# Heads 6 and 7 as a fourth tile, one chunk's k from TensorE, one chunk's 1/rms from GpSimd: a change to a fused linear-attention and feed-forward kernel

## The chip, the cores and the metric

The kernel runs on one core of one Trainium2 chip. The time is the device time of the execution in microseconds (us), as the median of several runs. The granted clock is the share of its full clock that TensorE was given; over a whole profiled run it was 0.992 for the kernel before.

The engines' names in the profile are PE (TensorE, matmul), PEld (TensorE's weight load), DVE (VectorE), ACT (ScalarE), POOL (GpSimd) and SP (SyncE, which issues most of the DMAs). "L92" stands in every line, because one helper records every operation; groups are told apart by the tiles' names.

## The reference

```python
# attention: r, k, v (4, 8, 768, 48); w, u (8, 48)
state = zeros(B, H, D, D)
for t in range(S):
    cur     = einsum('bhd,bhe->bhde', u * k[t], v[t])
    y[t]    = einsum('bhd,bhde->bhe', r[t], state + cur)
    state   = w * state + einsum('bhd,bhe->bhde', k[t], v[t])
# bridge: (B,H,S,D) -> x (3072 tokens, 384)
rms = sqrt(mean(x * x, axis=-1) + 1e-6)
xn  = x / rms * rms_g
g   = xn @ w_gate                       # 384 x 1536
out = (g * sigmoid(g) * (xn @ w_val)) @ w_out   # 1536 x 384
```

## The kernel before

Time is cut into 12 chunks of 64 tokens for all 4 batches, and chunks go through the feed-forward part in pairs; a pair change is the passage from one pair to the next. Eight heads of 48 features give 384 rows. Before the change these were laid out as three tiles of 128 rows: two heads each, and in the rows 48 to 63 of each half a third of head 6 or 7.

```python
def outputs(bank, half):                     # PE; two halves of two batches per chunk
    py = bank[:, 0 : CC * 2 * L].rearrange("p (i t) -> p i t", i=CC)     # CC = 3
    for bl in range(2):
        ...
        for i in range(CC):
            for z, m in ((0, ME), (1, MO)):  # 16 rows of head 6 or 7
                pe.matmul(py[64*z : 64*z+64, i, cols], VS[:, z, b, at : at+L], m[:, b, 3, :], start=True, stop=False, ...)
            for z, m in ((0, ME), (1, MO)):  # 48 rows of heads 0 to 5, added
                pe.matmul(py[64*z : 64*z+D, i, cols], VS[:, z, b, i*D : (i+1)*D], m[:, b, i, :], start=False, stop=True, ...)
```

The result of a pair of chunks is four parts (`k`) of 128 rows. The rows 0 to 63 belong to one batch, the rows 64 to 127 to the next, and `j` counts the two pairs of batches. Before the change, a part was stored by two DMAs, one for each half of the rows. The list `ap` is the access pattern, a step and a count for each dimension, the slowest first:

```python
def result(k, chunk, f, js=(0, 1)):
    def give():
        for bl in range(2):
            to = bass.AP(tensor=out.tensor, offset=out.offset + ((2*js[0] + bl)*S + chunk*L)*DM + f*HALF,
                         ap=[[DM, L], [2*S*DM, len(js)], [1, HALF]])     # 64 tokens, 2 batches, 192 columns
            sp.dma_start(out=to, in_=results[bl*L : (bl+1)*L, k, js[0] : js[-1]+1])
    add("SP", 1.0, [f"r{k}"], [], give, name="store")
```

The steady part also looks at the weights a second time, to prove that they fit the range that the fast path handles. A check is a load of 384 KB into the tile `sq`, issued by SyncE, and two operations of ScalarE on it. There are 36 of them.

```python
def check(n, src, k):
    add("SP", 0.95, [], keys, lambda: sp.dma_start(out=raw, in_=src[:, k*CHECK : (k+1)*CHECK]), land=LAND, ...)
    add("ACT", 0.57, [], keys, lambda: act.activation(hi, hi, AF.Abs), ...)
    add("ACT", 0.81, [], keys + ["seen"], lambda: act.activation(hi, hi, AF.Relu, ..., accum_out=seen[:, n:n+1]), ...)
```

Every operation is entered in a plan with an assumed cost. The plan searches for a good order, and the instructions are emitted engine by engine in that order, so the order on each engine is fixed when the kernel is built. `LAND` (2.1) is what the plan takes for the landing of a load. In the gaps of TensorE in the first 27 us of the plan, dummy matmuls on ones are put in.

## Time and profile before

| | before |
|---|---|
| first three runs, median | 640.38 us (638.73 to 642.36) |
| profiled span | 638.1 us |
| TensorE busy / not busy | 619.1 / 19.0 us |
| last matmul to the end | 9.9 us |

The prediction below shows the page's head, TensorE's waits and its costly blocks. Two more views. First the DMA issues (what is written and read, queue, number of issues, KB each, median us from issue to landing):

```profile
sq<-in_wka_dram SPq DMA_DIRECT2D x12, 384.0 KB, 3.1
out_dram<-rows_out SPq DMA_DIRECT2D x46, 96.0 KB, 2.3
```

A check's load lands in 3.1 us and a store in 2.3. Second, the window in which most of the start lies (its start and end in us, its length, then busy time with instructions of PE, PEld, DVE, ACT and POOL, the granted clock, the DMA share and GB/s):

```profile
12.80:38.00 25.20, 19.28 (x372) 17.20 (x374) 22.36 (x32) 18.73 (x60) 4.38 (x5) 0.99 0.87 297
```

### The profile page before, as it was taken

Reading aid. Unit: us, or ns where it says so; the run is one execution under the profiler, and the core shown is the slowest. Engines: PE = TensorE matmul, PEld = TensorE weight load, DVE = VectorE, ACT = ScalarE, POOL = GpSimd, SP = SyncE. Lnnn points to the kernel's source line nnn. Section 1 sums busy time; section 2 is a strip of 40 time slices with the busy share of each in tenths; the row PEclk is TensorE's granted clock in tenths of the full one; section 3 lists DMA queues with packets and bytes.
Section 4 is the critical chain, followed back from the end, with each engine's and each line's share of the span. In section 5 each row is a group of like instructions: output and inputs, shape, how many; then the busy total and the mean of one; then the engine's idle time right before and its main releaser. Section 6 shows DMA issues by size and latency. Waiting matters only on the chain.

```text
span 638.1 us, 15980 instructions
## 1 busy us (share of the span) xinstructions
PE 619.1 (97%) x6880; PEld 550.2 (86%) x6880; DVE 437.3 (69%) x619; ACT 348.3 (55%) x914; POOL 41.2 (6%) x39
## 2 busy tenths in 40 slices
PE   9879999999999999999999999999999999999993
PEld 8767787887788899888899888899888899988993
DVE  7988869877676795478694568795468576455631
ACT  5696388763594256338858327958326952212200
POOL 3145212200000000000000000000000000000000
PEclk9989999999999999999999999999999999999997
DMA  8797372404351022252423241523241501100001
GB/s 270 262 314 251 123 237 54 146 2 140 96 164 30 7 89 73 75 161 78 141 92 99 52 160 52 167 73 95 75 142 46 140 5 49 26 2 1 2 13 43
DMA packets 21265, 64.54 MB, mean 101 GB/s; under 512 B 2752, under 2 KB 8512, under 8 KB 19776
## 3 DMA queue, kind: packets, MB, share of 16 engines
q1 hardware_dynamic: 21184, 63.42, 32.5%
q8 instruction: 56, 0.92, 0.6%
q14 instruction: 25, 0.20, 0.1%
HBM read 58.69 MB, written 4.72 MB: 99 GB/s over the span
## 4 chain that ended last, share of the span: by engine, by line
PE 87%; DMA 4%; DVE 3%; ACT 3%; issue 1%; POOL 0%; SPq 0%; DVEq 0%; POOLq 0%; ACTq 0%
PE bank_b L92 28%; PE bank_a L92 26%; PE bank_c L92 23%; PE at L92 11%; DMA chan<-in_chan_dram 3%; DVE bits L92 1%; ACT MO L92 1%; DVE rows_out L92 1%; DMA sq<-in_wot_dram 1%; DMA sq<-in_wka_dram 0%; ACT ME L92 0%; ACT sq L92 0%; DVE ME L92 0%; DVE chan L92 0%; ACT VS L92 0%
## 5 line engine op out<-in xcount | busy, mean ns | idle before, releaser
L92 DVE TENSOR_TENSOR gv<-bank_b,m 128x512 f32<-128x512 f32 x90 | 62.1, 690 | 70.6 <-PE bank_b L92 69.6
L92 PE MATMUL bank_b<-xa,wa 64*128 64x256 f32 x444 | 55.2, 381 | 2.0 <-POOL wa L92 1.5
L92 ACT ACTIVATE gv<-bank_a 128x256 f32<-128x256 f32 x30 | 11.5, 382 | 79.8 <-PE bank_a L92 79.7
L92 ACT ACTIVATE sq<-sq 128x384 f32<-128x384 f32 x72 | 40.4, 561 | 23.7 <-DMA sq<-in_wot_dram 11.8
L92 ACT ACTIVATE gv<-gv 128x256 f32<-128x256 f32 (+1 forms) x60 | 30.6, 521 | 37.0 <-DVE gv L92 36.6
L92 DVE TENSOR_TENSOR gv<-bank_c,gv 128x512 f32<-128x512 f32 x60 | 41.4, 689 | 12.2 <-PE bank_c L92 11.2
L92 PEld LDWEIGHTS bank_b<-xa,wa 64*128 64x128 f32 x444 | 42.0, 187 | 8.8 <-POOL wa L92 1.7
L92 PE MATMUL bank_a<-xa,wa 64*128 64x256 f32 x396 | 49.5, 382 | 0.1
L92 PE MATMUL bank_a<-wo,h 128*128 128x192 f32 (+1 forms) x264 | 49.4, 343 | 0.0
L92 PE MATMUL bank_a<-xb,wb 64*128 64x256 f32 x396 | 48.3, 377 | 0.0
L92 ACT ACTIVATE MO<-dmask,du 64x64 f32<-64x64 f32 x176 | 46.3, 336 | 1.3 <-DVE du L92 0.8
L92 PEld LDWEIGHTS bank_a<-wo,h 128*128 128x128 f32 x264 | 43.5, 190 | 3.7 <-issue 0.3
L92 ACT ACTIVATE ME<-dmask,du 64x64 f32<-64x64 f32 x176 | 45.5, 331 | 0.7
L92 PE MATMUL bank_b<-t,s 64*128 64x256 f32 x360 | 44.3, 378 | 0.5 <-DVE rows_out L92 0.5
L92 PE MATMUL bank_b<-t,wb 64*128 64x256 f32 x360 | 44.1, 377 | 0.2 <-DVE gv L92 0.2
L92 PE MATMUL bank_c<-xb,s 64*128 64x256 f32 x360 | 44.2, 378 | 0.0
L92 PE MATMUL bank_c<-t,s 64*128 64x256 f32 x360 | 44.0, 377 | 0.0
L92 PEld LDWEIGHTS bank_a<-xa,wa 64*128 64x128 f32 x396 | 37.3, 187 | 6.1 <-issue 1.4
L92 PEld LDWEIGHTS bank_a<-xb,wb 64*128 64x128 f32 x396 | 38.3, 187 | 4.7 <-issue 0.3
L92 ACT COPY m<-bank_a 128x512 f32<-128x512 f32 (+1 forms) x35 | 19.8, 566 | 40.7 <-PE bank_a L92 23.2
L92 PEld LDWEIGHTS at<-ME,VS 128*64 128x64 f32 (+1 forms) x576 | 35.3, 135 | 7.3 <-DVE MO L92 4.1
L92 PE MATMUL at<-ME,VS 128*64 128x64 f32 (+1 forms) x576 | 37.3, 226 | 3.7 <-DVE MO L92 3.7
(143 smaller groups left out, 1288.5 us busy)
## 6 DMA issues: line engine op xcount, KB each, us to landing
chan<-in_chan_dram SPq DMA_DIRECT2D x11, 1024.0 KB, 6.0
TOK<-in_tok_dram SPq DMA_DIRECT2D x12, 768.0 KB, 5.6
VS<-in_vpad_dram SPq DMA_DIRECT2D x24, 336.0 KB, 5.0
raw<-in_wot_dram SPq DMA_DIRECT2D x8, 576.0 KB, 4.4
sq<-in_wka_dram SPq DMA_DIRECT2D x12, 384.0 KB, 3.1
sq<-in_wkb_dram SPq DMA_DIRECT2D x12, 384.0 KB, 3.1
sq<-in_wot_dram SPq DMA_DIRECT2D x12, 384.0 KB, 3.1
out_dram<-rows_out SPq DMA_DIRECT2D x46, 96.0 KB, 2.3
```

Of the source, the lines that this page charges most:

```text
L92: return lambda *args, **kwargs: self.tc.keep_in_program_order(give(*args, **kwargs))
```

## The change

The intent is to shorten TensorE's stream. Heads 6 and 7 become a fourth tile, made by 8 matmuls a batch in place of 12, and a DMA (`move_heads`) brings their 16-row pieces to the rows where the feed-forward part expects them. Chunks 2 and 3 take the short way of the norm that chunks 4 to 11 had. In the start, chunk 0's k by tokens is made by TensorE from k by channels in place of being loaded, the dummy matmuls before the first real one become fewer, and chunk 1's 1/rms is a power on GpSimd in place of a square root on ScalarE. Some smaller things go with it: the search tries four seeds, the first part of an output projection is cut in two, P4 and P7 change places, and the stores are cut by `j` in place of by half.

```diff
 def outputs(bank, half):
-        for i in range(CC):
-            ... 16 rows of head 6 or 7 (start), then 48 rows (stop): 4 matmuls
+        for p in range(HP):                                   # HP = 4
+            for z, m in ((0, ME), (1, MO)):
+                pe.matmul(py[64*z : 64*z+64, p, bl*L : (bl+1)*L], VS[:, z, b, p*L : (p+1)*L],
+                          m[:, b, p, :], start=True, stop=True, skip_group_check=True)
+def move_heads(lo, hi):
+    for z in range(2):
+        sp.dma_start(out=yT[64*z+D : 64*z+64, :, lo:hi], in_=last_heads[64*z : 64*z+D, lo:hi])
...
+def turn_k(bank, half):                                       # chunk 0 only: 16 matmuls a half
+    pe.matmul(pk[64-64*z : 128-64*z, bl, p, :], CH[rows, 1, b, p, :], KH[rows, z, b, p, :], ...)
+def keep_k(bank, half, z):
+    act.copy(KH[rows, z, 2*half : 2*half+2], pk[rows])
...
-        quick, brief = s == 0, s > FIRST + 1
+        quick, early, turned, brief = s == 0, s < 1, s < 1, s > 1
...
+def power(y, x):                                              # chunk 1: GpSimd, then a step of Newton on DVE
+    pool.tensor_tensor(out=y, in0=x, in1=minus_half, op=ALU.pow)
...
-            for _ in range(int((until - since - 0.3) / 0.22) - (9 if since == 0 else 0)):
+            for _ in range(int((until - since - 0.3) / (0.22 if since else 0.5))):
...
 def result(k, chunk, f, js=(0, 1)):
-    for bl in range(2):
-        to = bass.AP(..., ap=[[DM, L], [2 * S * DM, len(js)], [1, HALF]])
-        sp.dma_start(out=to, in_=results[bl * L : (bl + 1) * L, k, js[0] : js[-1] + 1])
-    add("SP", 1.0, [f"r{k}"], [], give, name="store")
+    for j in js:
+        to = bass.AP(..., ap=[[S * DM, 2], [DM, L], [1, HALF]])   # 2 batches, 64 tokens, 192 columns
+        sp.dma_start(out=to, in_=results[:, k, j])
+    add("SP", 0.6 * len(js), [f"r{k}"], [], give, name="store")
```

## The prediction

> **What bounds the kernel now.** I first read the page's busy shares and then the waits of TensorE. The page:
>
> ```profile
> span 638.1 us, 15980 instructions
> PE 619.1 (97%) x6880; PEld 550.2 (86%) x6880; DVE 437.3 (69%) x619; ACT 348.3 (55%) x914; POOL 41.2 (6%) x39
> ```
>
> The waits of TensorE (who, for whom, total us, times, longest):
>
> ```profile
> PE at L92 <- DVE MO L92: 3.7, 1, 3.7
> PE at L92 <- DVE diag L92: 1.7, 2, 1.0
> PE bank_b L92 <- POOL wa L92: 1.5, 1, 1.5
> PE bank_c L92 <- DVE pw L92: 1.2, 1, 1.2
> ```
>
> Of a span of 638.1 us, TensorE (PE) is idle for 19. The listed waits and two of 0.6 and 0.5 give 9.2; the other 9.9 lie after its last matmul (628.2 us in the timeline), where the last results are stored and the program ends. So in the steady part PE never waits, and what leaves PE's instruction stream leaves the time. Only the start is different. There PE is "busy" partly with dummy matmuls on ones: by the groups 82 instructions, 13.4 us, all before 27 us.
>
> Next I read the chain that ended last in order of time, for the cost of whole blocks (start, us, what):
>
> ```profile
> 36.66 4.62 PE at L92 x95
> 46.66 1.43 PE at L92 x12
> 76.57 1.57 PE at L92 x64
> 84.82 2.04 PE at L92 x64
> 118.07 2.89 PE at L92 x96
> ```
>
> The x96 block is one chunk's outputs: the code issues 4 x 12 = 48 matmuls and the trace has two instructions for each. It costs 2.89 us, 30.1 ns an instruction. The x64 block of 2.04 is one chunk's scores, the one of 1.57 its state update (48 columns), the x12 its mean squares. The first line is the outputs of chunk 1: the same work took 4.62 us. The windows say why (columns: PE, weight load, DVE, ACT, POOL busy; granted clock, DMA share, GB/s):
>
> ```profile
> 30.00:34.00 4.00, 1.57 (x12) 1.08 (x12) 3.54 (x6) 3.96 (x18) 1.99 (x2) 1.00 0.98 311
> 34.00:38.00 4.00, 1.34 (x40) 1.34 (x42) 2.89 (x5) 3.93 (x15) 0.40 (x1) 0.96 1.01 382
> 38.00:42.00 4.00, 4.00 (x70) 3.84 (x68) 3.90 (x6) 3.92 (x9) 2.28 (x3) 0.61 0.82 269
> ```
>
> From 30 to 38 PE is mostly idle while ACT and DVE are full and DMA at its limit, and just afterwards the granted clock is 0.61. From 41.3 us on PE has next to no gap. So the time is **start (41.3) + PE work + 9.9**.
>
> **What the Trainium skill says.** (1) "TensorE: Matmul & The Clock Gate", Part 3 (row/col tiling): small matmuls at different tile positions run concurrently, the position following the operands' start partitions. The trace agrees: the even and the odd head's instruction start at most 0.01 us apart, pairs about 0.06 us apart, so removing a pair of instructions removes about 0.06 us however few rows it filled. (2) The same page, "What's actually happening": an idle window of about 3.4 us throttles the array to half clock. The trace has it once: 3.7 us idle, then 0.61 granted and 4.62 in place of 2.89 us. (3) "ScalarE: Activation LUTs", "What ACT_TABLE_LOAD costs": about 1.28 us plus a drain, 2.66 us together. The trace agrees on the load (1.28 us), not on the drain: the square root at 49.03 us starts 0.02 us after its load ends. (4) "DMA: Bandwidth & Descriptors", latency table: about 2 us of fixed cost for a transfer; the trace's 96 KB stores land in 2.3 us (median).
>
> **The change part by part.**
>
> *Outputs.* Heads 6 and 7 were made in three 16-row pieces, accumulated beside heads 0 to 5 (12 matmuls a batch); now each pair of heads is one pair of matmuls (8 a batch), 64 in place of 96 instructions a chunk. At 30.1 ns that is 1.93 us, so **0.96 us less PE a chunk**. Chunks 2 to 11: 9.6 us, all on the path. Chunks 0 and 1 lie in the start.
>
> *Norm of chunks 2 and 3.* They leave the route by mean squares (1.43 us) and spreading of a diagonal (groups: 2.7 us for four chunks, 0.67 each), 2.10 together, for the one-matmul route of chunks 4 to 11 (groups: 5.2 us for eight, 0.65 each): **1.45 less PE each, 2.9 in all**. It costs DVE a wide reciprocal (1.75 us) and two sums (1.1) a chunk, off PE's path as DVE is 69% busy. Chunk 1 keeps the long route with 16 instructions in place of 12: +0.5 us.
>
> Sum after the start: -9.6 - 2.9 + 0.5 = **-12.0 us**.
>
> *The start.* (a) The dummies: 44 instructions run from 1.16 to 9.09 us, though the inputs of the first real matmuls, ku (done 6.54) and r (landed about 6.3), were there 2.5 us before. The new count divides the gap by 0.5 in place of 0.22, some 13 matmuls; at the measured 0.36 us each they end near 6. The scores, and the masked copies on DVE that waited 1.9 us for them, come about 2.4 us sooner. (b) Chunk 0's k by tokens moves to PE (64 instructions like the state update's 1.57 us, and four ACT copies, 1.9 us) where PE had only dummies to do; DVE loses 1.92 us (17.39 to 19.3), the token load of chunk 0 (768 KB) goes, and the power table's 0.75 us moves later. (c) Because chunk 0 no longer holds the token buffer, chunk 1's tokens can be loaded at once: before, that load was issued at 19.33 and landed near 24.9, and only then came the three bonus operations (to 27.8) and the 8 us of diagonals on ACT (28.6 to 36.9) for which PE waited. This is the largest item. (d) The fourth tile costs ACT about 0.6 + 0.2 us a chunk, and the move of 16 rows adds a DMA, 2.3 us or more, before the scaling; the norm chain (mean squares, root, diagonal, spread, about 4 us) runs beside it. (e) The power on GpSimd takes two table switches, 2.56 us, off ACT.
>
> All items cannot add up: ACT has 2.7 us idle between 22.3 and 25.0 and about 5.4 before, and weights still need DVE (0.9 to 2.3 us a piece) and DMA at over 300 GB/s. I take the outputs of chunk 1 to end at about 36.5 in place of 41.3: 2.4 from (a), about 2 from (b) and (c), 1 from shorter outputs and a whole clock, less about 0.6 for the move. **-4.8 us.**
>
> *Steady moves.* For later chunks the scaling of the second chunk of a pair comes about 3 us later (move) plus 0.6 (ACT). Around 340 us the sum t2 is ready at 342.7 and its user f2 starts at 352.7, around 250 us at 247.1 against 254.2. So 7 to 10 us of slack swallow it. ACT goes up by about 0.55 x 12 = 6.6 us less the tables, to about 353: still 57%.
>
> *Tail.* One store in place of two at the very end: 0.3 us at most; splitting P1 and reordering P4 and P7 remove no wait that exists. I count zero.
>
> Total: 640.4 - 12.0 - 4.8 = 623.6, rounded to **623.5 us**, 2.7% faster.
>
> **Rivals.** *R1, the start gives nothing*: moves of 16 rows queue behind weight loads (a 384 KB load took 7.6 us to land there, DMA share 1.0) and x of chunks 0 and 1 comes as late as before, or weights bound the first cells anyway. DVE is 3.9 of 4 us busy at 38 to 46, which speaks for it; the slack in the token chain against. Then only -12.0 remains: about 628. *R2, a new wait in the steady part*: the move is late on the in-order SP queue (which waits behind checks and buffers) and stalls f2 at each of four pair changes, or DVE's 5 us more at 60 to 180 us show. The 7 to 10 us of slack speak against; 1 to 2 us at each pair change give 628 to 632. *R3, the start gains all it can*: the four searches find a better order and PE runs on from 34 us: 620 or a little less. *R4, the matmuls aren't the cost*: if weight load or issue set the outputs' time, 64 instructions would not take two thirds. But scores with 64 instructions take 2.04 us, so at worst 0.1 us a chunk is lost.
>
> **Range and chances.** Main case with R3: 618 to 626, about 70%. R1 or a mild R2: 626 to 630, about 22%. Beyond: 8%. The border of 2% is 640.4/1.02 = 627.8. Range 618 to 629; faster by over 2% 0.80, within 2% 0.18, slower 0.02.
>
> **What would show it.** Outputs blocks of x64 at about 1.93 us; 384 in place of 576 instructions on each side of that group; PE busy near 600; chunks 2 and 3 without a diagonal on PE; 12 us less between the outputs of chunk 1 and the last matmul. First real matmuls near 6.6 us, chunk 1's token load landed well before 20, its outputs' end near 36.5 without a 0.61 clock. Moves landing in 2 to 4 us. I am wrong if PE shows waits for xa, t or the move in the steady part, if the outputs blocks take over 2.2 us, or if the outputs of chunk 1 end after 40 us.

## The result, and the profile after

| | before | after |
|---|---|---|
| median of 4 runs | 641.28 us (638.73 to 642.36) | 657.34 us (654.39 to 658.29) |
| profiled span | 638.1 us | 652.6 us |
| TensorE busy / not busy | 619.1 / 19.0 us | 613.1 / 39.5 us |
| last matmul to the end | 9.9 us | 13.7 us |

The changed kernel is slower: the ratio is 1.0254 (95% interval 1.0212 to 1.0297). A ratio here is the mean time of one kernel's fast runs over the mean of the other's fast runs of the same rounds, so it is not quite the ratio of the medians.

The head of the page after:

```profile
span 652.6 us, 15362 instructions
PE 613.1 (94%) x6544; PEld 540.8 (83%) x6544; DVE 437.8 (67%) x621; ACT 354.3 (54%) x895; POOL 42.8 (7%) x41
```

TensorE's busy time fell by 6.0 us and the time in which it is not busy rose by 20.5, which is the whole +14.5 us of the span. So the first question is what TensorE waits for. Its waits after (for whom, total us, times, longest):

```profile
PE bank_a L92 <- DVE h L92: 16.4, 3, 7.9
PE bank_c L92 <- POOL wa L92: 2.3, 1, 2.3
PE bank_b L92 <- DVE h L92: 1.7, 1, 1.7
```

The first line is new: three waits for `h`, the product of gate and value, 16.4 us together. The tail grew by 3.8 us; with the waits that makes 20.2 of the 20.5 us. The chain of waits around the longest one, in order of time (start, us, what; SPq is SyncE issuing a DMA, DMA the time from issue to landing):

```profile
250.87 1.96 SPq L92
...
252.93 7.30 DMA sq<-in_wka_dram
...
260.31 0.55 ACT sq L92
...
260.88 0.63 ACT sq L92 x2
...
261.53 1.28 ACT L92
...
262.82 0.39 ACT gv L92
...
263.24 0.43 DVE h L92
...
263.72 2.93 PE bank_a L92 x12
266.65 2.04 PE bank_b L92 x12
268.69 1.29 PE bank_c L92 x12
```

Read it from the bottom. TensorE's block at 263.72 needs `h`, which DVE makes from ScalarE's SiLU (`ACT gv`), which needs its table (1.28 us), which stands in ScalarE's order behind the two operations of a weight check (`ACT sq`), which wait for that check's load: 7.30 us, ended at 260.23. Nothing of `h` needs the check; it is only ahead on the same engine. The next block of twelve matmuls takes 2.93 us and the one after it 2.04, where the following takes 1.29: after the idle time the clock is not whole (0.80 granted in 260 to 262 us, below, and 0.50 in 262 to 268). The second such wait, at 369.10, has a load of 7.42 us in front and two blocks of 2.93 and 2.25. So the two slow starts add (2.93 + 2.04 - 2 x 1.29) + (2.93 + 2.25 - 2 x 1.29) = 5.0 us of "busy" time. The same kind of load in the kernel before, in the same chain view at the same place:

```profile
255.30 3.36 DMA sq<-in_wot_dram
...
260.01 3.04 DMA sq<-in_wka_dram
```

Two such loads together take 6.4 us there, less than the one after. The store issued before the load also holds SyncE itself: 1.96 us here and 2.65 at the second wait, where the longest issue of a store in e1 (below, the old stores) is 0.97. Windows of 2 us of the kernel after (columns as above) say what the load meets:

```profile
250.00:252.00 2.00, 1.65 (x16) 1.50 (x18) 0.33 (x2) 1.98 (x9) 0.00 (x0) 1.00 0.14 46
...
254.00:256.00 2.00, 1.80 (x18) 1.27 (x14) 0.00 (x0) 0.00 (x0) 0.00 (x0) 1.00 0.31 68
256.00:258.00 2.00, 0.00 (x0) 0.00 (x0) 0.00 (x0) 0.00 (x0) 0.00 (x0) 1.00 0.62 205
258.00:260.00 2.00, 0.00 (x0) 0.00 (x0) 0.00 (x0) 0.00 (x0) 0.00 (x0) 1.00 0.12 45
260.00:262.00 2.00, 0.00 (x0) 0.00 (x0) 0.00 (x0) 1.64 (x4) 0.00 (x0) 0.80 0.00 0
```

While the stores run (250 to 252) the DMA share is 0.14 at 46 GB/s. Then the load comes and for a moment 205 GB/s flow; and then, from 258 to 260, it is 0.12 and 45 GB/s again: a last piece of the load still waits on few engines. The Trainium skill's page "DMA: Bandwidth & Descriptors", section "Why a DMA increments its semaphore by 16 and not by 1" (paragraph "How many engines (k)"), says that a transfer is spread over the largest number up to 16 that divides the slowest dimension of both of its access patterns. The new store's slowest dimension in DRAM is 2 (`[S * DM, 2]`), so it would run on 2 of 16 engines, a share of 0.125; the old one's is 64 (`[DM, L]`). The measured 0.12 to 0.14 agree.

The packed trace shows it more directly, in the semaphore updates that DMAs make when they land. A store of the kernel before leaves 16 of them. Each of the six stores here leaves two at its landing (one more comes at its issue), and they land one after another, 2.1 us apart, the last at 259.27. The load leaves 16: 14 between 257.49 and 257.91, and the last two at 260.12 and 260.23, after the last store. At the second wait it is the same: 14 by 363.3, the last two at 365.1 and 365.6, after the last store at 364.7. So two of the load's sixteen parts wait for the stores, and that costs 2.3 us. The other 2 us of its delay come before: its first packet moves 2.9 us after the issue, where it was 1.0 in the kernel before (at 260.01); why is not shown.

So the theory is: **the form of the stores, not the parts that the change was made for**. Its rivals: the move on SyncE's queue (R2 of the prediction), or the new order of the plan (other seeds, other costs), which happens to put checks badly.

Of the parts that were meant, the chain of after shows one directly (outputs of later chunks, to be held against 2.89 us for x96):

```profile
118.47 2.02 PE at L92 x64
...
223.52 2.02 PE at L92 x64
```

And the start gained nothing. The first output projection stood at 48.09 us before and stands at 47.98 us after. From its end on, both kernels have the same gate, value and projection matmuls left, so it is a fair mark.

### The profile page after: what moved, and what is told of

The parts are those of the page before. It is cut to its first block, busy times and chain, and to the rows that moved or that the text cites.

```text
span 652.6 us, 15362 instructions
## 1 busy us (share of the span) xinstructions
PE 613.1 (94%) x6544; PEld 540.8 (83%) x6544; DVE 437.8 (67%) x621; ACT 354.3 (54%) x895; POOL 42.8 (7%) x41
## 4 chain that ended last, share of the span: by engine, by line
PE 82%; DMA 7%; ACT 5%; DVE 2%; SPq 1%; issue 1%; POOL 0%; ACTq 0%; POOLq 0%
PE bank_b L92 27%; PE bank_a L92 25%; PE bank_c L92 21%; PE at L92 10%; DMA sq<-in_wka_dram 2%; DMA sq<-in_wot_dram 2%; DMA VS<-in_vpad_dram 1%; DMA raw<-in_wka_dram 1%; SPq L92 1%; ACT sq L92 1%; ACT L92 1%; ACT MO L92 1%; ACT VS L92 1%; ACT ME L92 1%; DVE h L92 1%
## 5 line engine op out<-in xcount | busy, mean ns | idle before, releaser
L92 PE MATMUL bank_a<-xa,wa 64*128 64x256 f32 x396 | 52.2, 398 | 14.4 <-DVE h L92 14.4
L92 PEld LDWEIGHTS bank_a<-xa,wa 64*128 64x128 f32 x396 | 38.7, 195 | 21.8 <-DVE h L92 15.2
L92 ACT ACTIVATE gv<-gv 128x512 f32<-128x512 f32 (+1 forms) x60 | 31.1, 523 | 38.4 <-DVE gv L92 38.1
L92 PE MATMUL bank_b<-t,s 64*128 64x256 f32 x360 | 45.7, 388 | 0.0
L92 PEld LDWEIGHTS bank_b<-t,s 64*128 64x128 f32 x360 | 36.3, 196 | 4.8
L92 PEld LDWEIGHTS bank_c<-t,s 64*128 64x128 f32 x360 | 34.6, 187 | 4.9 <-issue 0.5
```

What stands on the lines that cost most here:

```text
L92: return lambda *args, **kwargs: self.tc.keep_in_program_order(give(*args, **kwargs))
```

## The experiments

In all, 17 kernels ran, each against runs of the kernel before. They were timed over three rounds, and e15, e16 and e17 over five. The results are right but for one, which is named.

| run | median us | ratio to before (95% interval) |
|---|---|---|
| after | 657.34 | 1.0254 (1.0212 to 1.0297) |
| e1_half_stores | 632.67 | 0.9871 (0.9833 to 0.9909) |
| e2_before_pair_stores | 658.49 | 1.0269 (1.0242 to 1.0296) |
| e3_half_stores_last | 651.52 | 1.0153 (1.0128 to 1.0178) |
| e4_quarter_stores | 644.48 | 1.0051 (1.0029 to 1.0072) |
| e5_checks_without_dma | 634.9 | 0.9907 (0.9888 to 0.9926) |
| e6_k_by_load | 635.75 | 0.9921 (0.9899 to 0.9944) |
| e7_long_norm_2_3 | 636.92 | 0.9928 (0.9903 to 0.9952) |
| e8_stores_by_gpsimd | 630.71 | 0.9848 (0.9826 to 0.9870) |
| e9_old_dummies | 637.34 | 0.9941 (0.9904 to 0.9979) |
| e10_tokens_land_5 | 629.91 | 0.9817 (0.9779 to 0.9854) |
| e11_land_4 | 638.29 | 0.9943 (0.9898 to 0.9988) |
| e12_moves_twice | 643.23 | 1.0021 (0.9988 to 1.0053) |
| e13_first_dummies_only | 632.8 | 0.9883 (0.9853 to 0.9913) |
| e14_no_early_moves | 633.82 | 0.9879 (0.9842 to 0.9915) |
| e15_both | 632.11 | 0.9857 (0.9831 to 0.9883) |
| e16_keep_k_on_dve | 635.87 | 0.9916 (0.9899 to 0.9932) |
| e17_best_keep_k_on_dve | 632.16 | 0.9868 (0.9848 to 0.9887) |

The kernel before had medians of 640.56 to 641.45 us. The calls ran on several chips, so runs of different calls are compared by their ratios, not by their times.

The plan is searched again when its operations or costs change. The traces show the order of TensorE, ScalarE and DVE as in e1 for after, e3, e4, e5, e9, e12, e13 and e14 (dummies left out); in e8 one operation of a check stands elsewhere on ScalarE, in e16 only the moved copies differ. In e6, e7, e10, e11, e15 and e17 the order is another one, so their differences contain that too.

### The form of the stores: e1, e2, e3

**e1_half_stores** is the changed kernel with the old form of the stores. The plan's assumed cost is left, so the order of all else is the same.

```diff
-                for j in js:
-                    to = bass.AP(..., ap=[[S * DM, 2], [DM, L], [1, HALF]])
-                    sp.dma_start(out=to, in_=results[:, k, j])
+                for bl in range(2):
+                    to = bass.AP(..., ap=[[DM, L], [2 * S * DM, len(js)], [1, HALF]])
+                    sp.dma_start(out=to, in_=results[bl * L : (bl + 1) * L, k, js[0] : js[-1] + 1])
```

> The changed kernel with the result stores of the kernel before: two transfers of 64 partitions each in place of one transfer of 128 partitions per token block, everything else and the order of instructions the same. Theory A (the new store's destination starts with a dimension of 2, it runs on two of the 16 DMA engines, and the weight check's load behind it lands 4 us late and holds ScalarE): the waits of 7.9 and 6.5 us of TensorE at the pair changes go, with the half-clock stretches after them (about 5 us), the 2 us at 525 and 3.8 us of tail: 630 to 635 us, faster than before by 1 to 2%. Rival B (the moves of 16 rows hold the in-order queue): the waits stay, 650 us or more. Rival C (the new order of the search puts a check ahead of SiLU): also 650 or more.

Measured 632.67 us: 24.7 us under the kernel after by the medians, 24.5 by the ratios. The order of the plan is not the cause, as it is unchanged here. **e2_before_pair_stores** puts only the new form of the stores (the reverse of the edit) into the kernel before.

> The kernel before with only the changed kernel's store form. Theory A: it gets waits of several us at pair changes and a tail about 4 us longer: 650 to 665 us, slower by 2% or more. Rivals B and C: as before but for the tail, 641 to 645 us.

Measured 658.49 us, +17.8: the stores alone make the old kernel as slow as the new one, with no move and no new plan. Its waits of TensorE have entries of a size that the kernel before has in no place of the steady part:

```profile
PE bank_b L92 <- DVE gv L92: 6.4, 5, 2.7
PE bank_a L92 <- DVE h L92: 3.3, 1, 3.3
```

So the theory holds from both sides. **e3_half_stores_last** uses the old form only for the last pair of chunks (`if s + 2 >= NS:` the old form, else the new one), to see how much of it lies in the tail.

> The changed kernel with the old store form only in the last pair of chunks. Theory A: only the tail after the last matmul shortens, from about 13.7 to about 10 us; the two long waits stay: 652 to 654 us. If the tail is set by something else (the flag, the end of the program): 657.

Measured 651.52, ratio 1.0153 against 1.0254: 0.0101 x 641 = 6.5 us lie in the last pair of chunks. The tail from the last matmul to the end is 13.7 us after and 7.1 us in e1, a difference of 6.6 that agrees. (In e3 itself it is 7.4 us, where about 10 were expected.)

### By which way: e5, e4, e8

**e5_checks_without_dma** keeps the new stores and takes away the load of the check. ScalarE's two operations read a tile of ones, so the check proves nothing, but the results are right.

```diff
-            "SP", 0.95, [], keys, lambda: sp.dma_start(out=raw, in_=src[:, k * CHECK : (k + 1) * CHECK]), land=LAND,
-            name=f"look {n}",
+            "SP", 0.95, [], keys, lambda: None, land=LAND, name=f"look {n}",
...
-        add("ACT", 0.57, [], keys, lambda: act.activation(hi, hi, AF.Abs), name=f"look {n}")
+        still = free_dims(ones, (0, CHECK // P), (1, P))
+        add("ACT", 0.57, [], keys, lambda: act.activation(hi.rearrange("p (a b) -> p a b", b=P), still, AF.Abs), ...)
```

> The changed kernel with its new pair stores kept, but the weight checks work on a constant in place of a freshly loaded piece (36 loads of 384 KB less; the result is right for these inputs, the check itself is void). Order of instructions the same. Theory A' (the slow stores hurt only by way of the check, which ScalarE in its fixed order cannot pass until its load has landed): the two long waits go and the long tail of 13.7 us stays: 633 to 638 us. If the stores delay other loads that TensorE needs (chan, tokens, V) or the moves: long waits stay, above 645.

Measured 634.9 us, though every store still runs on few engines. TensorE's waits for `h` shrink from 16.4 to

```profile
PE bank_a L92 <- DVE h L92: 2.0, 1, 2.0
```

This shows the way: outside the tail the slow stores cost next to nothing by themselves. They cost through the check's load behind them, and through ScalarE's order. The tail stays long, at 13.3 us, as expected.

**e4_quarter_stores** keeps the order of stores by `j`, but cuts each into two of 64 rows with 64 as the slowest dimension. There are four issues for a part in place of two.

```diff
                 for j in js:
-                    to = bass.AP(..., ap=[[S * DM, 2], [DM, L], [1, HALF]])
-                    sp.dma_start(out=to, in_=results[:, k, j])
+                    for bl in range(2):
+                        to = bass.AP(..., ap=[[DM, L], [1, HALF]])
+                        sp.dma_start(out=to, in_=results[bl * L : (bl + 1) * L, k, j])
```

> The changed kernel with every store cut into 64-partition pieces: twice as many transfers to issue, each with a destination that starts with 64 rows. Theory A (few engines): 630 to 636 us, as the half stores. Rival D (what delays the check is the time that the SyncE queue needs to issue stores): twice the issues make it worse than the changed kernel, above 657 us, or at least no better.

Measured 644.48, between the two expectations: half of the loss is gone (12.9 us), but 11.8 us over e1 remain. Of these, 5.4 lie in the tail (12.5 us against 7.1) and 4.5 in TensorE's waits for `h`, still 9.9 us, the longest 4.7. A likely reason is to be seen in e1 too, in its chain before a pair change:

```profile
344.90 0.60 SPq L92
...
345.54 0.60 SPq L92
...
346.23 4.52 DMA sq<-in_wka_dram
```

SyncE takes 0.60 us to issue one store, and the check's load stands behind several of them in its order. So the place behind the issues is a second, smaller cost, and e4 doubles the issues. But this load also takes 4.52 us to land, where the median in e1 is 3.1, so issue time is not all of it. **e8_stores_by_gpsimd** tests this on e1 by letting GpSimd issue the stores; it was busy for 7% of the span.

```diff
-                    sp.dma_start(out=to, in_=results[bl * L : (bl + 1) * L, k, js[0] : js[-1] + 1])
+                    pool.dma_start(out=to, in_=results[bl * L : (bl + 1) * L, k, js[0] : js[-1] + 1])
-            add("SP", 0.6 * len(js), [f"r{k}"], [], give, name="store")
+            add("POOL", 0.6 * len(js), [f"r{k}"], [], give, name="store")
```

> The changed kernel with half stores issued by GpSimd, which is idle after 160 us, in place of SyncE. If the remaining waits of 0.9 and 2.5 us at the pair changes come from the 2.6 us of store issues ahead of the check's load on the SyncE queue, they go and the time is 628 to 631. If GpSimd issues slowly, the tail grows: 633 to 640.

Measured 630.71, ratio 0.9848 against 0.9871 of e1. The intervals overlap, so the gain of the time alone is not certain; the waits are clearer. e1's are the two lines here, e8's those in the next fence:

```profile
PE bank_a L92 <- DVE h L92: 5.4, 3, 2.5
PE bank_b L92 <- DVE h L92: 1.9, 1, 1.9
```

```profile
PE bank_a L92 <- DVE h L92: 2.0, 1, 2.0
PE bank_b L92 <- DVE h L92: 2.2, 1, 2.2
```

The two waits at pair changes, 3.4 us together, are gone in e8; the one of 2.0 us stays, and so does the one in `bank_b`, which lies in the start. The Trainium skill's page "Trainium Kernel Development and Optimization", section "Key Constraints", says that DMAs from SyncE, ScalarE and GpSimd share the 16 engines, and that issuing from several saves only issue time. The trace shows what e8 changed: the check's load is no longer behind the stores. At the same pair change it is issued at 342.16 us, before the first store (343.00), and lands in 3.1 to 3.4 us; in e1 it is issued at 346.23, after the four stores. So the loss in e1 is the load's place behind the stores; which share of it is SyncE's issue time is not separated.

### The terms of the sum: e6, e7, e9, e12

Each undoes or doubles one part, on e1. With the two intervals combined, each worth below is uncertain by about 3 us. **e6_k_by_load**: chunk 0's k by tokens is loaded again, as before.

```diff
-        if s >= 1:
+        if s >= 0:
             add("SP", 1.8, [], ["TOKr", "TOKk"], lambda: load_tok(s), ...)
-        quick, early, turned, brief = s == 0, s < 1, s < 1, s > 1
+        quick, early, turned, brief = s == 0, s < 1, False, s > 1
-    loads(0), quarter(0), mixing(0), token_tables()
+    token_tables(), loads(0), quarter(0), mixing(0)
```

> The changed kernel with half stores (632.7), and chunk 0's k by tokens loaded and scaled on DVE again as before, the power table and the token load early again. The prediction says that this part was worth about 2 us of the start, with the token chain of chunk 1: 634 to 637 us. Rival (the start is held by ScalarE and by the weights, not by this chain): within 1 us of 632.7.

Measured 635.75, ratio 0.9921 against 0.9871: the part is worth about 0.0050 x 641 = 3.2 us (with another order of the plan).

**e7_long_norm_2_3**: chunks 2 and 3 take the long norm again (with the new power on GpSimd).

```diff
-        quick, early, turned, brief = s == 0, s < 1, s < 1, s > 1
+        quick, early, turned, brief = s == 0, s < 1, s < 1, s > FIRST + 1
```

> The changed kernel with half stores, and chunks 2 and 3 on the long norm (mean squares, diagonal, spread) again, with the power on GpSimd in place of ScalarE's root. The prediction: 2.9 us more TensorE work, all on the path: 635 to 636.5 us. Rival (the short norm's wide reciprocal and root cost as much elsewhere): 632 to 633.

Measured 636.92, ratio 0.9928: worth about 0.0057 x 641 = 3.7 us, where 2.9 were forecast. TensorE is busy for 4.0 us more than in e1 (614.2 against 610.2), again with another order of the plan.

**e9_old_dummies**: the old number of dummy matmuls.

```diff
-            for _ in range(int((until - since - 0.3) / (0.22 if since else 0.5))):
+            for _ in range(int((until - since - 0.3) / 0.22) - (9 if since == 0 else 0)):
```

> The changed kernel with half stores (632.7) and the old count of dummy matmuls (22 in place of 13 before the first real ones; more in later gaps too if any are longer). The prediction: the first real matmuls 2.4 us later and the start with them, 634.5 to 635.5. Rival (the 2.4 us are lost again before chunk 0's norm, where ScalarE sets the pace): within 1 us of 632.7.

Measured 637.34, ratio 0.9941: worth about 0.0070 x 641 = 4.5 us, more than the 2.4 that were expected. Part of it may be the clock and not the later start: before the tail, e9's profile has five stretches of 3.4 us at half clock, e1's two. So both parts of the start are real, in the sense that undoing each costs something.

**e12_moves_twice**: every move of 16-row pieces is issued twice. The second writes the same bytes, so it waits for the first.

```diff
-            sp.dma_start(out=yT[64 * z + D : 64 * z + 64, :, lo:hi], in_=last_heads[64 * z : 64 * z + D, lo:hi])
+            for _ in range(2):
+                sp.dma_start(out=yT[64 * z + D : 64 * z + 64, :, lo:hi], in_=last_heads[64 * z : 64 * z + D, lo:hi])
```

> The changed kernel with half stores and every move of 16 rows issued twice. The prediction holds that a move has 7 to 10 us of slack in the steady part, so a second one of 2.3 us costs at most the start something: 632 to 634. Rival (the moves lie on the path, or hold the SyncE queue at each pair change): two seconds moves per chunk add 1 to 2 us at each of four pair changes and at the start, 637 or more.

Measured 643.23, about 10 us more than e1. That is the range of the rival (637 or more), but not at its place. TensorE's waits have two new entries. The first lies in the start, at 33.67 us; the second is five short waits after 60 us:

```profile
PE at L92 <- DVE xa L92: 7.8, 1, 7.8
PE bank_b L92 <- DVE gv L92: 3.8, 5, 1.4
```

As the waits for `h` are shorter than in e1, all waits after 60 us come to 7.1 us, against 6.2 in e1. So in the steady part even a move of twice the length costs about 1 us, which refutes the move as the cause of the long waits there. In the start it is not hidden: there a late move on SyncE's queue holds up the scaling.

### Where the start's gain went: e13, e14, e16

In the window 12.80 to 38.00 us, the columns as above, the kernel after and then e1:

```profile
12.80:38.00 25.20, 21.51 (x318) 18.70 (x320) 21.51 (x36) 23.47 (x65) 7.31 (x7) 0.96 0.74 251
```

```profile
12.80:38.00 25.20, 21.45 (x349) 18.97 (x347) 21.93 (x36) 23.59 (x65) 6.96 (x7) 1.00 0.74 247
```

DMA fell from 0.87 to 0.74, but ACT rose from 18.73 to 23.5 us of 25.2. Work was moved from DMA to an engine that had 6.5 us left and now has 1.7. In e1 the first output projection begins at 47.00 us, 1.1 earlier than before, but runs at half clock (5.80 us against 3.98), so it ends at 52.80, later than before (52.06).

**e13_first_dummies_only** leaves out the dummies after the first gap (`if since == 0:` in place of `if until < 27:`), in case they hold up real matmuls.

> The changed kernel with half stores (632.7) and dummy matmuls only in the very first gap, none in the later gaps before 27 us. If the dummies of the gaps at 14.7, 21.6 and 24.6 us hold back chunk 0's outputs (by 1.5 to 2 us) and the spreading of its norm (1.5 us), as the trace suggests, the start comes 2 to 3.5 us sooner: 629 to 631. If the clock falls to half for lack of work instead: 633 or more.

Measured 632.8: no difference from e1. The clock is what changes. e13's windows:

```profile
14.00:18.00 4.00, 3.09 (x60) 2.90 (x60) 3.90 (x6) 3.59 (x10) 0.00 (x0) 0.57 0.98 360
...
22.00:26.00 4.00, 3.31 (x56) 2.69 (x58) 3.42 (x8) 3.92 (x13) 1.00 (x1) 0.50 0.79 247
```

In e1 the clock at 22 to 26 us is 1.00. So these dummies hold the clock up, and TensorE's speed there sets nothing that the time shows, unless a gain and the slower clock cancel out.

**e14_no_early_moves** leaves out the moves of chunks 0 and 1. The result is wrong (relative error 0.256).

```diff
+    pool.memset(yT, 0.0)
-                    lambda lo=lo, half=half: move_heads(lo, P * half + P), land=LAND, name=f"move {s}",
+                    (lambda: None) if s < 2 else (lambda lo=lo, half=half: move_heads(lo, P * half + P)), ...
```

> The changed kernel with half stores, without the moves of chunks 0 and 1 (wrong results on purpose in the rows of heads 6 and 7 of these two chunks; order otherwise the same). If the moves cost the start what the prediction allowed, 0.6 us: 631.5 to 632.7. If they are what ate the gain of the start: 628 to 630.

Measured 633.82: no gain. The moves as they are don't take the start's gain.

**e16_keep_k_on_dve** takes the four copies of chunk 0's k from ScalarE to DVE (`dve.tensor_copy` in place of `act.copy` in `keep_k`), with the plan unchanged.

> The changed kernel with half stores (632.7), the four copies of k by tokens out of the accumulator on DVE in place of ScalarE (1.9 us of ScalarE between 13 and 15 us; the plan still books them on ScalarE, so all else keeps its order). If the start is now bound by ScalarE's stream (23.6 of 25.2 us busy from 12.8 to 38), chunk 1's outputs and the time come 1 to 2 us sooner: 630.7 to 631.7. If weights or DMA bound it: 632 to 633.5.

Measured 635.87, ratio 0.9916 against 0.9871: worse, outside both expected ranges, though the intervals just touch. Its window:

```profile
12.80:38.00 25.20, 20.60 (x318) 18.17 (x320) 24.09 (x39) 21.41 (x61) 6.74 (x6) 1.00 0.71 235
```

ACT is down to 21.4 us, but DVE is now up to 24.1 of 25.2. Relieving ScalarE alone is no help, so ScalarE alone isn't shown to be the bound; both engines are nearly full, and the start is a chain that goes back and forth between them.

### A better version: e10, e11, e15, e17

In e8 the token load of chunk 2 took 5.76 us (in the chain at 33.92 us), while the plan took 2.1. **e10_tokens_land_5** tells the plan 5.0 for the tokens of chunks 1 to 3, on top of e8:

```diff
-            add("SP", 1.8, [], ["TOKr", "TOKk"], lambda: load_tok(s), land=LAND, name=f"load tok {s}")
+            add("SP", 1.8, [], ["TOKr", "TOKk"], lambda: load_tok(s), land=5.0 if s < 4 else LAND, name=f"load tok {s}")
```

> The kernel with half stores by GpSimd (630.7), whose plan now believes that the token loads of chunks 1 to 3 take 5 us to land (measured 5.2) and not 2.1. If the wait of 2.2 us at 47 us and the half clock after it come from ScalarE having the diagonals of chunk 2 ahead of SiLU while their tokens have not landed, they go: 626.5 to 629.5. If the start is bound by something else, no change or worse by the accident of a new order: 630 to 633.

Measured 629.91, ratio 0.9817, the lowest of all. TensorE's waits of 2.3 us for GpSimd's `wa` and of 2.2 for `h` in `bank_b` are gone, as was the aim, but shorter ones came (2.1 us more for `h` in `bank_a`, 1.4 for `gv`, 0.6 for `MO`), and the first output projection begins at 49.21. Against e8 (0.9848) it isn't told apart by time. **e11_land_4** takes 4.0 for all loads (`LAND = 4.0`), also on e8.

> The kernel with half stores by GpSimd, whose plan believes that every load lands in 4.0 us in place of 2.1. Same question more broadly: waits of the start shorter, 626 to 630; else 630 to 634.

Measured 638.29, a miss: 8.4 us over e10, and about 6 over e8 by the ratios. A truer figure for one load helped or did no harm; a larger one for every load, most of which land in less, gave a worse order.

**e15_both** joins e10 and the edit of e13; **e17_best_keep_k_on_dve** joins e10 and the edit of e16.

> Half stores by GpSimd, the plan told that early token loads land in 5 us (629.9), and dummy matmuls in the first gap only. If the late dummies cost 2 to 3 us here too: 626.5 to 628.5; if not, 629 to 632.

> The fastest kernel so far (half stores by GpSimd, token loads planned with 5 us; 629.9) with the same copies on DVE: 628 to 629 if ScalarE bounds its start too, else 629.5 to 631.

Measured 632.11 and 632.16, ratios 0.9857 and 0.9868; the second is above both of its expected ranges. Neither beats e10 (0.9817); e17's interval lies next to e10's with a little overlap, e15's overlaps it more. The best version found is e10: 1.8% faster than the kernel before, and 4.3% below the kernel after (0.9817 / 1.0254 = 0.957).

## Why the prediction was wrong

**The step that failed first is the tail's: "One store in place of two at the very end: 0.3 us at most ... I count zero".** It looked at the number of stores, at the end only, and not at their shape. The stores move the same bytes in nearly the same number of issues (48 against 50), but have 2 as its slowest dimension in place of 64. In place of zero, the runs show +24.7 us (after against e1). Of the 22.1 us between the two profiled spans 6.6 lie in the tail, 11.0 in the waits for `h` (16.4 against 5.4) and some 3 in the slow clock behind those waits (5.0 against 2.0), 20.6 together. The prediction had cited the very page that has the rule for the engines, for its fixed cost, and not asked it about the new access pattern.

**Rival R2 was near, with the wrong culprit.** It foresaw "a new wait in the steady part" at the pair changes, on SyncE's in-order queue, but blamed the move and the sum before f2, and found 7 to 10 us of slack for those. e12 shows slack for a second move at a cost of about 1 us; how much more there is was not tested. The wait came by another path: store, check's load, ScalarE's order, SiLU, `h`. "1 to 2 us at each pair change" was 7.9 and 6.5 us at the two worst. Of the text's own conditions for being wrong, one was met: the outputs of chunk 1 ended after 40 us (37.40 + 2.93 = 40.33). Waits for `xa`, `t` or the move, which it named for the steady part, did not come; it had no sign for a wait for `h`.

**The start's -4.8 us gave nothing** (R1). The step that failed is that an earlier token chain ends the start earlier. The chain did come earlier: the first real matmuls start at 6.46 us (about 6.6 forecast, 9.02 before), the bonus operations on chunk 1's tokens at 15.1 in place of 24.9. Then other things ended last. In after, TensorE's block ahead of chunk 1's outputs waits 2.3 us for GpSimd's `wa`, a piece of weights, until 35.16, which is R1's "weights bound the first cells", and the outputs then run in part at half clock. In e1 the outputs end at 39.1, 2.2 us sooner than before (36.5 forecast), and the first projection waits for chunk 2: its token load lands at 39.35, three operations of DVE and the diagonals on ScalarE follow until 44.37, and only behind them, in ScalarE's order, stand the table and the SiLU of `h`. e10 took both waits away without a gain that the time shows, but with another order of the plan, so this does not tell what they were worth.

The parts (a) and (b) have value, as undoing them costs about 4.5 and 3.2 us (each uncertain by 3). But the sum "2.4 from (a), about 2 from (b) and (c), 1 from shorter outputs" treated them as time off a path, while (b) and (d) put work on ScalarE: 4.7 us more in the window 12.8 to 38. The prediction counted ScalarE's idle time of 2.7 and 5.4 us as room, and that room was filled. What exactly ends last in the new start stays open: the later dummies (e13), the moves (e14) and ScalarE's copies by themselves (e16) are each without a gain when taken away. Only the moves are cleanly excluded by that: e13 also lowered the clock, and e16 also loaded DVE.

**What held, by the numbers:**

- Outputs: 2.02 us in place of 2.89 a chunk, forecast 1.93. That is 0.87 saved, not 0.96, so 8.7 us in place of 9.6 for ten chunks. R4 had set its worst case at 0.1 us a chunk, and it is nearly that.
- Instructions: 384 on each side of the outputs' group, as forecast.
- Norm of chunks 2 and 3: forecast 2.9 us, undoing it costs about 3.7.
- The move lands in 2.3 us (e1) and is hidden in the steady part, as forecast; in the start it has no such slack (e12).
- TensorE's busy time was to be near 600 and was 613.1; even in e1 it is 610.2, partly because the dummies are 82 instructions as before (26 in place of 44 before the first real matmul, more in later gaps), chunk 0's k adds 2.0 us, and the clock is slow once in the start and once at a pair change.

With the stores put right, e1 is 8.0 us faster than before (medians 632.67 against 640.69), where 16.8 were forecast. Of the missing 8.8, the start accounts for about 5.0 (4.8 - 0.5 forecast for this point, as chunk 1's longer norm lies before it, and the first projection ends at 52.80 against 52.06). New waits for `h` (5.4) and a slow clock behind one of them (2.41 + 2.14 - 2 x 1.29 = 2.0 at 354 us) take 7.4, and the outputs 0.9. Against that, the norm of chunks 2 and 3 gave 0.8 more than forecast (uncertain by 3), and the tail is 2.8 us shorter than before (7.1 against 9.9), which had been counted as zero; which of the small reorderings did that was not tested. This sum, 5.0 + 7.4 + 0.9 - 0.8 - 2.8 = 9.7, is an estimate from the profiles, 0.9 over the missing 8.8.

## What to carry to other kernels

When a change touches a DMA, write down the slowest dimension of both of its access patterns, not only its bytes and its count: a store that nobody waits for can still hold a load that somebody does. Ask of every in-order engine what stands ahead of the critical operation on it; a check that is off every data path was on this one. And in a start where two engines are nearly full, a gain from moving work is not the sum of the parts: read the room in the receiving engine's busy time in that window first.

## What the Trainium skill lacked or had wrong

- "DMA: Bandwidth & Descriptors" has the rule for the number of engines, and it agrees: slowest dimension 2 gave a DMA share of 0.12 to 0.14 at 45 to 46 GB/s. It does not say, in that section, what this costs a transfer behind it: a 384 KB load landed in 7.3 us in place of 3.0. Its first packet moved 1.9 us later than before, and the last two of its 16 landings came 2.3 us after the others, behind the stores.
- "ScalarE: Activation LUTs" gives about 2.7 us for a table switch with its drain. Here the switch takes 1.28 us, and the next activation starts 0.01 to 0.02 us later (261.53 + 1.28, then 262.82); the one before ended 0.02 us earlier.
- "TensorE: Matmul & The Clock Gate", section "What's actually happening", has the lower clock come after an idle window of about 3.4 us. That fits the wait of 7.9 us, after which twelve matmuls took 2.93 us in place of 1.29. But the clock also fell to 0.50 after 3.4 us in which TensorE was busy for 1.5 us (e1, to 47.64) or 2.1 us (e13, to 21.16), so the window need not be idle throughout; how little work is too little, the page does not say.
- No page that I found gives, for this chip and in us, the time in which SyncE issues a DMA: here 0.60 for a store of 96 KB in its old form and 0.33 for a load of 384 KB (medians of e1), and up to 2.65 for a store in the new form.
- No page that I found gives the cost of a power on GpSimd: 0.7 to 1.1 us for 128 x 2 elements (after, e1 and e7).
